# Four single-chunk units at the start, integer addition on VectorE, another order of the gate chain and three more rooms for raw weights, in a linear-attention and SwiGLU kernel

## The chip, the cores and the metric

The kernel runs on one core of one Trainium2 chip. The metric is device microseconds (us) of one execution, as a median of several executions. PE is TensorE, DVE is VectorE, ACT is ScalarE, POOL is GpSimd, SP is SyncE; a "q" behind the name (SPq) marks an instruction that issues a transfer.

## The reference, cut to what matters

```python
# attention: batch 4, heads 8, sequence 768, head size 48, float32
mag = sqrt(a_re**2 + a_im**2)
scale = minimum(mag, 0.999) / (mag + 1e-6)
a_re_n, a_im_n = a_re * scale, a_im * scale
for t in range(S):                                  # complex decay of a state
    new_re = ar * S_re - ai * S_im
    new_im = ar * S_im + ai * S_re
    S_re, S_im = new_re + k[t] outer v[t], new_im
    y[t] = q[t] @ S_re
# feed-forward: 3072 tokens, 384 -> 1536 -> 384
xn = x / sqrt(mean(x * x) + 1e-6) * rms_g
g, val = xn @ w_gate, xn @ w_val                    # weights come as float64
out = (g * sigmoid(g) * val) @ w_out
```

The weights arrive in eight bytes per number and are narrowed on the chip.

## The kernel before

The sequence is cut into 24 chunks of 128 positions. A *unit* is one or two chunks whose gates (magnitude, angle, sine, cosine, running product) DVE and ACT compute together. The rotated k and q are moved by DMA into another layout, PE makes scores, states and outputs, and each double chunk then goes through the feed-forward part (FFN). The weights come in 18 *pieces*: six of w_gate, six of w_val, six of w_out. A raw piece lies in a *room* until ACT and DVE have narrowed it.

The units, one gate chain (shortened), the decays, and the narrowing of a piece:

```python
units = [(0, 1), (1, 1)] + [(n, UC) for n in range(2, N, UC)]    # two of one chunk, then double
...
# gate chain of one unit, each line one step for one engine
yield E("DVE", ..., lambda: tt(im, im, y), K("t0"))              # angle work is mixed in
yield E("DVE", ..., lambda: tt(w, s, r))                         # magnitude
...
yield E("ACT", ..., lambda: act_(out=im, in_=im, func=AF.Arctan), table=["atan"])
yield E("DVE", ..., products, K("p"))                            # running products of the gates
yield E("DVE", ..., sums, K("sums"))                             # running angle
yield E("ACT", ..., lambda: act_(out=r, in_=p, func=AF.Abs_reciprocal_sqrt), table=["ars"])
...
yield E("DVE", ..., [K("k")], lambda t=t: tt(t["k"], t["k"], t["r"]))
yield E("DVE", ..., [K("q")], lambda t=t: tt(t["q"], t["q"], t["p"]))
for i, (o, x, f) in enumerate((("ks", "k", s), ("k", "k", y), ("qs", "q", s), ("q", "q", y))):
    yield E("DVE", ..., lambda ...: tt(t[o], t[x], f), *names)   # four rotation products
...
def decays(...):                                   # a trip through memory, both ways on SyncE
    nc.sync.dma_start(out=dec..., in_=ends[:, u, :, 0:m])
    for a in range(2):
        nc.sync.dma_start(out=t["decay"][a * D:(a + 1) * D, :, 0:m], in_=dec...)
yield step("SP", 1.3, [("p", u)], decays, mb=0.02, then=2.5, queue="rows", ends=[("rows", u)])
...
def total(...):                                    # last step of a weight piece
    nc.gpsimd.tensor_tensor(out=to, in0=part["t"], in1=to, op=ALU.add)
```

No engine's program is written by hand. A small list scheduler inside the kernel, the class `Order`, takes the next step of every lane, estimates when it could begin, emits the earliest, and so fixes the sequence of instructions of each engine when the kernel is built. Its constants are guesses of durations, among them the transfer rate in MB per us:

```python
class Order:
    HOP = 0.06
    ISSUE = 0.6
    LAND = 1.9
    RATE = 0.2
    ...
            if "mb" in more:
                queue = more.get("queue", "rows")
                self.moved[queue] = max(self.moved.get(queue, 0.0), at + 0.4) + more["mb"] / self.RATE
                end = self.moved[queue] + self.LAND
```

## Time and profile before

| | before |
|---|---|
| median of 3 executions | 834.41 us (832.93 to 840.13) |
| span of the profiled run, mean granted clock | 829.0 us, 0.947 |
| first score of chunk 0 / 2 / 4 begins | 43.2 / 138.5 / 177.2 us |
| first gate/value tile of the FFN | 78.6 us |
| last output product ends | 821.9 us |
| PE busy from 200 to 600 | 392.5 of 400 us |

In the page's rows of digits one character stands for a fortieth of the span, about 20.7 us, and a 9 means busy for 90% or more. A timeline line gives start, duration, engine, source line, operation, output and inputs, shapes, count, and in brackets the idle time before it with what ended it.

### The profile page before, as it was taken

What the parts mean: (1) busy time and instruction counts of PE and PEld (TensorE: products, weight loads), DVE (VectorE), ACT (ScalarE), POOL (GpSimd) and SP (SyncE); (2) the same over time, 40 slices, a digit from 0 to 9 for tenths busy, and PEclk for the clock granted to TensorE, in tenths of its full rate; (3) what the DMA queues carried; (4) which work ended last, traced back from release to release, by engine and by line L of the source; (5) the groups of instructions that cost most, each with busy time, mean ns of one, the idle gap of its engine ahead of it and who ended that gap; (6) DMA issues with size and microseconds to landing.
All of it is one profiled execution on the core that took longest, in us unless ns stands there. A gap on an engine that the chain in (4) does not pass through costs nothing.

```text
span 829.0 us, 12028 instructions
## 1 busy us (share of the span) xinstructions
PE 761.3 (92%) x4820; PEld 609.9 (74%) x4820; DVE 428.7 (52%) x709; ACT 360.8 (44%) x565; POOL 79.6 (10%) x103
## 2 busy tenths in 40 slices
PE   5079967989998999999999999999999999999996
PEld 2067845778886878988678888678888778886783
DVE  4656999857775766857784766122211213320220
ACT  5632475557675767767664775111111101110110
POOL 6434432200000000000010000000000000000000
PEclk9556987989998999999999999999999999999999
DMA  8929637562647276554635470045100106200510
GB/s 198 204 54 225 158 114 115 125 113 52 103 96 125 49 127 107 125 74 99 78 106 77 124 116 1 8 97 132 52 0 1 58 13 193 81 1 27 177 63 23
DMA packets 100976, 76.48 MB, mean 92 GB/s; under 512 B 39665, under 2 KB 89585, under 8 KB 100913
## 3 DMA queue, kind: packets, MB, share of 16 engines
q1 hardware_dynamic: 98128, 69.74, 39.9%
q0 software_dynamic: 1920, 5.51, 3.0%
q8 instruction: 40, 0.66, 0.4%
q10 hardware_dynamic: 864, 0.39, 0.2%
q14 instruction: 24, 0.19, 0.1%
HBM read 51.98 MB, written 4.76 MB: 68 GB/s over the span
## 4 chain that ended last, share of the span: by engine, by line
PE 76%; DMA 8%; DVE 7%; ACT 3%; SPq 2%; issue 2%; POOL 1%; DVEq 0%; ACTq 0%; POOLq 0%
PE gv_ps L1160 39%; PE out_ps L1184 20%; PE s_ps L1014 5%; PE y_ps L1087 5%; PE state_ps L1057 3%; SPq L861 2%; DMA hT<-in_w_gate_dram 2%; DMA qr<-q 2%; PE ss_ps L1110 2%; DMA qr<-qs 1%; PE kt_ps L1035 1%; DMA raw<-in_w_gate_dram 1%; DMA dec<-ends 1%; PE ss_ps L1123 1%; DMA raw<-in_w_out_dram 1%
## 5 line engine op out<-in xcount | busy, mean ns | idle before, releaser
L1160 PE MATMUL gv_ps<-xT,wg 128*128 128x256 f32 x864 | 213.8, 384 | 0.2
L1160 PE MATMUL gv_ps<-xT,wv 128*128 128x256 f32 x864 | 210.3, 379 | 0.0
L1184 PE MATMUL out_ps<-wo,hT 128*128 128x384 f32 x576 | 195.9, 493 | 7.8 <-POOL wo L968 7.8
L1160 PEld LDWEIGHTS gv_ps<-xT,wg 128*128 128x128 f32 x864 | 163.5, 192 | 26.1 <-issue 1.4
L1160 PEld LDWEIGHTS gv_ps<-xT,wv 128*128 128x128 f32 x864 | 164.6, 190 | 22.5
L1184 PEld LDWEIGHTS out_ps<-wo,hT 128*128 128x128 f32 x576 | 107.6, 191 | 76.3 <-POOL wo L968 9.6
L612 DVE TENSOR_TENSOR hT<-gv_ps,hT 128x256 f32<-128x256 f32 x144 | 59.6, 421 | 191.3 <-ACT hT L1164 191.0
L1164 ACT ACTIVATE hT<-gv_ps 128x256 f32<-128x256 f32 x144 | 54.1, 383 | 210.4 <-PE gv_ps L1160 209.8
L1014 PE MATMUL s_ps<-qr,kr 96*128 96x128 f32 x384 | 57.0, 310 | 45.3 <-DMA kr<-k 33.0
L1014 PEld LDWEIGHTS s_ps<-qr,kr 96*128 96x128 f32 x384 | 53.0, 221 | 48.7 <-issue 48.6
L1120 POOL TENSOR_TENSOR rs<-ssq,mhalf 128x1 f32<-128x1 f32 x24 | 18.5, 773 | 582.0 <-DVE ssq L1115 582.0
L1193 ACT COPY ot<-out_ps 128x384 f32<-128x384 f32 x24 | 11.5, 480 | 63.8 <-PE out_ps L1184 63.8
L615 DVE SCALAR_TENSOR_TENSOR xT<-y_ps,gcol,rb 128x128 f32<-128x128 f32 x72 | 20.7, 343 | 35.8 <-ACT rb L1128 29.9
L1019 DVE TENSOR_TENSOR am<-s_ps,causal 128x512 f32<-128x512 f32 x48 | 32.1, 683 | 13.2 <-PE s_ps L1014 12.7
L1057 PEld LDWEIGHTS state_ps<-vz,kt 128*96 128x96 f32 x320 | 32.2, 176 | 1.6 <-issue 0.7
L1164 ACT ACT_TABLE_LOAD x25 | 32.1, 1283 | 0.4
L1057 PE MATMUL state_ps<-vz,kt 128*96 128x48 f32 x320 | 32.1, 257 | 0.0
L1128 ACT COPY rb<-ss_ps 128x128 f32<-128x128 f32 x24 | 6.3, 264 | 59.1 <-PE ss_ps L1123 59.1
L1039 ACT COPY kt<-kt_ps 128x384 f32<-128x384 f32 x40 | 17.4, 478 | 26.4 <-PE kt_ps L1035 26.4
L1087 PE MATMUL y_ps<-am,vz 128*32 128x128 f32 x768 | 27.6, 287 | 0.0
L990 DVE TENSOR_REDUCE least__113<-raw 128x1 f32<-128x768 f32 x18 | 17.0, 944 | 20.0 <-DMA raw<-in_w_out_dram 16.2
L1110 PEld LDWEIGHTS ss_ps<-ones,sq 128*128 128x128 f32 x144 | 20.3, 202 | 8.5 <-ACT sq L1105 5.0
(113 smaller groups left out, 818.1 us busy)
## 6 DMA issues: line engine op xcount, KB each, us to landing
raw<-in_w_out_dram SPq DMA_DIRECT2D x12, 768.0 KB, 4.5
k<-in_k_dram SPq DMA_DIRECT2D x24, 192.0 KB, 3.3
q<-in_q_dram SPq DMA_DIRECT2D x24, 192.0 KB, 3.9
vz<-in_v_dram SPq DMA_DIRECT2D x24, 192.0 KB, 4.5
out_dram<-ot SPq DMA_DIRECT2D x24, 192.0 KB, 2.6
raw<-in_w_gate_dram SPq DMA_DIRECT2D x6, 768.0 KB, 4.6
raw<-in_w_val_dram SPq DMA_DIRECT2D x6, 768.0 KB, 4.5
re<-in_a_re_dram SPq DMA_DIRECT2D x33, 128.0 KB, 3.0
```

The costliest lines, as they stand in the source:

```text
L612: nc.vector.tensor_tensor(out=o, in0=x, in1=y, op=op)
L615: nc.vector.scalar_tensor_tensor(out=o, in0=x, scalar=c, in1=y, op0=op0, op1=op1, **kw)
L1014: nc.tensor.matmul(u["s_ps"][a][:, h], lhsT=u["k"][:, a * HH + h], rhs=u["q"][:, a * HH + h], start=True, stop=True)
L1019: nc.vector.tensor_tensor(out=u["am"][a], in0=u["s_ps"][a], op=ALU.mult, in1=causal.unsqueeze(1).to_broadcast([C, HH, C]))
L1039: nc.scalar.copy(out=u["kt"][a], in_=u["kt_ps"][a])
L1057: nc.tensor.matmul(u["st_ps"][:, h], lhsT=u["kt"][h // HH][:, h % HH], rhs=u["v"][:, h, 0:D], start=True, stop=True)
L1087: nc.tensor.matmul(u["y_ps"][32 * p:32 * (p + 1), j], lhsT=columns(left, j, odd, p), rhs=right(h), start=side == 0 and i == 0, stop=side = ...
L1110: nc.tensor.matmul(u["ss_ps"][:, 0:1], lhsT=u["sq"][:, d], rhs=ones, start=d == 0, stop=d == ND - 1)
L1120: nc.gpsimd.tensor_tensor(out=u["rs"], in0=u["ssq"], in1=mhalf, op=ALU.pow)
L1160: nc.tensor.matmul(ps[:, i], lhsT=w_[:, f * P // FW, d, cols], rhs=t["xT"][:, d], start=d == 0, stop=d == ND - 1)
L1164: nc.scalar.activation(out=t["hT"][:, f], in_=t["gv", f][:, 0], func=AF.Silu)
L1184: nc.tensor.matmul(t["o_ps", i], lhsT=t["hT"][:, f, i * C:(i + 1) * C], rhs=wo[:, f], start=f == 0, stop=f == NF - 1)
```

## The change

The intent: chunks 2 and 3 no longer form one double unit but two single ones, so that they can go on through DVE and ACT early. GpSimd no longer adds integers, so it no longer holds up DVE. The products of the gate magnitudes come ahead of the angles, so that k and q are scaled earlier. Raw pieces also use the room of the out-projection weights, which are not there yet. The moves alternate between k and q, three raw pieces instead of six leave at the start, and the scheduler gets one common transfer clock at rate 0.22 in place of one per queue at 0.2. The core of the diff:

```diff
-    RATE = 0.2
+    RATE = 0.22
...
-                queue = more.get("queue", "rows")
-                self.moved[queue] = max(self.moved.get(queue, 0.0), at + 0.4) + more["mb"] / self.RATE
-                end = self.moved[queue] + self.LAND
+                self.moved = max(self.moved, at + 0.4) + more["mb"] / self.RATE
+                end = self.moved + self.LAND
...
-    units = [(0, 1), (1, 1)] + [(n, UC) for n in range(2, N, UC)]
+    ONES = 4
+    units = [(n, 1) for n in range(ONES)] + [(n, UC) for n in range(ONES, N, UC)]
...
+    GL = 0.3
+    GU = (0.0, 0.05, 0.7, 0.7)      # lateness of the gate lanes of units 0 to 3
...
             # gate chain: products first, then angles; k and q scaled ahead of the angle sums
+            yield E("DVE", tt_us(n1), [K("k")], lambda t=t: tt(t["k"], t["k"], t["r"]))
+            yield E("DVE", tt_us(n1), [K("q")], lambda t=t: tt(t["q"], t["q"], t["p"]))
             ... sums, fraction, sine, cosine ...
-            for i, (o, x, f) in enumerate((("ks", "k", s), ("k", "k", y), ("qs", "q", s), ("q", "q", y))):
+            for i, (o, x, f) in enumerate((("ks", "k", s), ("qs", "q", s), ("k", "k", y), ("q", "q", y))):
...
-    EARLY = 6
+    EARLY = 3                       # pieces fetched from GpSimd's queue at the start
...
-        two = (0, 1) if i < 2 else (2, 3) if i < 2 * NW and i % 4 > 1 else (4, 5)
+        k = i if i < 2 else 2 + (i - 2) % 5 if i < 2 * NW else 7 + i % 2    # rooms 4 to 6 lie in wo
...
-                nc.gpsimd.tensor_tensor(out=to, in0=part["t"], in1=to, op=ALU.add)
+                tt(to, part["t"], to, ALU.add)
...
+                        for _ in range(7):           # dummies on rotated data before the first score
+                            nc.tensor.matmul(flat(u["s_ps"][a])[:, 0:ND * C], lhsT=ident, rhs=rotated, ...)
```

## The prediction

> **What bounds the kernel now.** I read the page's table of forty slices first, then the busy times by stretch, then the timelines of TensorE (PE) and VectorE (DVE), then the SyncE queue. From the page:
>
> ```profile
> PE   5079967989998999999999999999999999999996
> DVE  4656999857775766857784766122211213320220
> PEclk9556987989998999999999999999999999999999
> DMA  8929637562647276554635470045100106200510
> ```
>
> A slice is 20.7 us. From the tenth slice on PE is full at full clock; only the first nine show holes and a clock near half. The stretches, with bounds put at stage changes (columns: stretch, its length, busy us of PE, PEld, DVE, ACT, POOL with instruction counts, granted clock, DMA share, GB/s):
>
> ```profile
> 0.00:43.20 43.20, 10.77 (x21) 4.56 (x21) 25.28 (x55) 26.21 (x45) 24.74 (x61) 0.69 0.96 197
> 43.20:78.60 35.40, 30.08 (x201) 24.76 (x202) 18.14 (x27) 9.71 (x17) 13.01 (x9) 0.55 0.61 130
> 78.60:109.60 31.00, 31.00 (x145) 27.31 (x144) 28.83 (x33) 16.19 (x24) 14.15 (x8) 1.00 0.63 154
> 109.60:138.40 28.80, 16.25 (x33) 6.97 (x32) 28.04 (x30) 19.00 (x24) 8.78 (x4) 0.84 0.63 120
> 138.40:177.20 38.80, 36.45 (x299) 29.07 (x299) 29.09 (x46) 24.87 (x36) 4.35 (x3) 0.94 0.63 118
> ```
>
> 43.2 us pass before the first score; 35.4 go into the attention of chunks 0 and 1 at clock 0.55; 31.0 are the first gate/value group, clean; in the next 28.8 PE has nearly nothing to do, while DVE is busy 28.0 of them.
>
> How much useful PE work is there? Warm lengths from PE's timeline: 144 gate/value tiles of 2.6 us (374), 24 output rows of 7.75 (186), 24 score groups of 1.85 (44), 44 output sides of 0.95 (42), 20 states of 1.32 (26), 20 transposes of 0.7 (14), 24 norms of 1.0 (24): **710 us**. By t = 200 these are done: 18 tiles (46.8), 48 of 576 output records at 0.323 (15.5), six scores (11.1), eleven sides (10.4), five states and five transposes (10), the norms (5.5): about **99 us**. So 101 us are lost before 200; afterwards 611 us of work take 622 (200 to 822), a loss of 11, and 7 us are tail. The change can only win from the 101.
>
> The timeline shows what the loss is made of:
>
> ```profile
> 43.17 3.75 PE L1014 MATMUL s_ps<-qr,kr 96*128 96x128 f32 x16 [29.77 <-DMA kr<-k]
> ...
> 116.08 2.92 PE L1184 MATMUL out_ps<-wo,hT 128*128 128x384 f32 x4 [4.99 <-POOL wo L968]
> 121.84 2.27 PE L1184 MATMUL out_ps<-wo,hT 128*128 128x384 f32 x4 [2.83 <-POOL wo L968]
> 123.90 9.77 PE L644 MATMUL s_ps<-causal,ident 128*128 128x512 f32 x20
> 138.45 3.76 PE L1014 MATMUL s_ps<-qr,kr 96*128 96x128 f32 x16 [4.77 <-DMA dec<-ends]
> ```
>
> The first score waits for moved rows and runs cold (3.75 us against 1.98 warm at t = 143). After the first group PE waits for converted out-projection weights, fills with dummy products, and gets chunk 2 only at 138. The cause is on DVE: chunks 2 and 3 are one double unit that begins at 39.5 and shares DVE with all 18 weight pieces.
>
> **What the Trainium skill says, and whether this trace agrees.** (1) "SBUF — State Buffer", Who interferes with whom: a VectorE instruction with two SBUF inputs and a GpSimd one that reads SBUF exclude each other for the whole instruction. Agreed: beside a GpSimd weight addition DVE operations of 0.95 us show two to three times that:
>
> ```profile
> 120.15 2.46 DVE L612 TENSOR_TENSOR k<-k,r 128x768 f32<-128x768 f32 x1
> 122.53 0.95 DVE L612 TENSOR_TENSOR q<-q,p 128x768 f32<-128x768 f32 x1
> ...
> 119.33 2.46 POOL L968 TENSOR_TENSOR wo<-t,wo 128x768 int32<-128x768 int32 x1 [3.30 <-DVE wo L615]
> ```
>
> (2) "TensorE: Matmul & The Clock Gate", What's actually happening: an idle window of about 3.4 us halves the PE clock, a sustained busy one restores it. Agreed: 3.75 against 1.98. The dummies of 2.65 to 13.4 are wasted, since 30 us of idleness follow. (3) "ScalarE: Activation LUTs", What ACT_TABLE_LOAD costs: about 1283 ns a load, plus a drain. The load agrees (25 in the largest group, mean 1283); the drain is no separate row. (4) "DMA: Bandwidth & Descriptors", Issuing engines are not separate DMA queues: all issuers share 16 engines. Agreed: in the first 43 us the share is 0.96 at 197 GB/s, and chunk 0's last move (q) needs 7.3 us behind weight pieces.
>
> **The change part by part.**
>
> *Integer addition on VectorE.* Removes 18 GpSimd additions (1.81 to 2.53 us). Each visibly stretches one DVE operation by about 1.2 to 1.6 us (2.06, 2.17, 2.40, 2.46, 2.57 against 0.55 or 0.95). Adds 18 DVE operations of 0.95 (the row of the `or`, same shape), pitch 0.87. DVE: 18 x (0.9 - 1.3), about -7 us; near even. Latency of a piece falls by about 1 us.
>
> *Four single-chunk units.* Chunks 2 and 3 can begin early, in parallel lanes. Cost: a 384-wide operation has a pitch of 0.47 on DVE, a 768-wide one 0.87, so two singles cost 0.07 more on each of 17 operations: +1.2 us, plus some small scans and copies: +2 us. ACT likewise.
>
> *Gate products ahead of angles.* Chunk 0 loads three tables between 17 and 25.6 before (arctan, reciprocal root, sine); now the root follows while its table is in, and arctan and sine can share one: two of 1.28 saved, about 2.6 us. Work on k and q starts earlier. I put the last rotation of chunk 0 at 25 (28.8 before). Later units save loads too, off the path.
>
> *Transfers.* Three weight pieces instead of six go out early: 2.3 MB less ahead of the moves, 11 us at 200 GB/s; v is postponed; k moves before q. The q move, 4 instead of 7.3 us, no longer starts behind raw pieces. First score: 25 + 2 issue + 5 landing, about **33** instead of 43.2. Three more rooms in the output weights give seven pieces in flight. DMA was nearly idle from 48 to 58 (0 to 2 GB/s in the finer slices), so the postponed pieces have room there.
>
> *Seven dummies on the rotated data* instead of twenty early ones warm PE during the move. Scores through norms of chunks 0 and 1 are about 13 us warm and took 25 (30.1 less 4.9 of dummies). With dependency gaps I expect 20 to 24 us instead of 35.4: first gate/value tile near **55 to 58** instead of 78.6.
>
> *Then weights set the pace.* DVE work until four chunks, all 18 pieces and group 0 are through: 4 units of 11 (two took 22 of the 25.3 busy us before 43.2) = 44; 18 pieces at 0.47 + 0.87 + 0.87 = 40; masks, states and norms 3.15 per chunk = 13; 12 gate products 4.5. Sum **101 us**. DVE starts at 8.3; with 12 us of holes (27 in the same phase before) it is through at about 121. DMA gives the same: 14.2 MB of weights and 1.8 MB for each of four chunks (with moves) are 21.4 MB, 107 us at 200 GB/s.
>
> *The sum.* At 121, PE can have done four chunks (25), group 0 (31) and its output (15.5) = 72 useful us, so 50 are lost. From then on group 1 and two output rows give 46 us of supply, against about 35 for the next double unit (DVE 23, moves and decays 10): no new hole. Total 710 + 50 + 11 + 7 = 778 as the ideal. I add 18 for stalls at handovers, pieces that do not come in the right order, and cold stretches: a span of 796, and 4 for the median's offset from the span (834.4 against 829.0 before): **800 us**. It would be 34 us or 4% less.
>
> **Rivals.** (a) *VectorE becomes the sole bound* between 55 and 120: pieces take 2.2 of DVE, two pieces 4.4 per pair of tiles, which last 5.2 on PE, so group 0 nearly fills DVE and chunks 2 and 3 starve until near 115. For it: DVE is at 28.8 of 31.0 already. Then the hole after group 0 moves rather than closes: loss of 75, 825 us. Against: 20 us of earlier start, during which the extra lanes use idle DVE. (b) *Weights arrive late*: nine pieces wait for chunk 1's rotation, and SyncE issues in order (1.9 us a move, 2 to 2.9 a piece). Group 0 then stretches from 31 to 40: +9, about 810. (c) *The early gain is hidden*: the later chunks arrive no earlier, so the FFN waits later. Then 820 to 830. Against: DVE has 27 idle us before 78.6 that more units can fill. (d) *Everything fits*: 780 to 785.
>
> **Range and chances.** From the ideal 778 plus half the handover allowance to rival (b) plus a partial (a): **784 to 818**. More than 2% faster means below 817.7. Chances: faster 0.86, same 0.12, slower 0.02. Slower would need a later steady state worse than before, which nothing in the change adds.
>
> **What would show each step.** First score at 30 to 36, in about 1.9 us; first gate/value tile before 60; no GpSimd additions and no DVE operations of 2 us and more; chunk 2's score before 110 instead of 138; dummies far fewer near 124; PE full from about 125; DVE idle below 15 us between 8 and 120. It would be wrong if PE still idles 20 us after group 0, if group 0 takes over 45, or if new waits appear past 200, where I assume 18 with the tail, as now.

## The result, and the profile after

| | before | after |
|---|---|---|
| median | 833.67 us (830.48 to 840.13, 4 runs) | 859.00 us (856.78 to 860.44, 4 runs) |
| span, clock of the profiled run | 829.0, 0.947 | 857.9, 0.957 |
| first score of chunk 0 / 1 / 2 / 3 / 4 | 43.2 / 52.0 / 138.5 / 143.2 / 177.2 | 47.7 / 59.5 / 104.9 / 115.0 / 182.1 |
| first / twelfth gate/value tile begins | 78.6 / 107.1 | 81.0 / 151.4 |
| first output row begins | 109.6 | 166.9 |
| last output product ends | 821.9 | 848.7 |

The kernel became slower: the ratio is 1.029 with a 95% interval from 1.022 to 1.036. A ratio is the mean time of one kernel's fast runs over the mean of the other's in the same rounds, so it is not quite the ratio of the medians quoted. Executions over 1.5% slower than the fastest of the same kernel are left out of the means. Results are correct.

The rows of the page of the kernel after (a slice is 21.4 us):

```profile
PE   0265789989998989999998979999999999999995
DVE  2866858957666757575775558323211112320220
PEclk9977879998998999999999989999999999999998
```

PE is not full until the seventh slice (128 us), and there is an 8 in the fifteenth and twenty-second slice and a 7 in the twenty-fourth, between 300 and 515 us, where the kernel before had only 9s. The stretch from 400 to 500 shows that later loss. Columns are stretch, its length, busy us of PE, PEld, DVE, ACT and POOL with counts, granted clock, DMA share and GB/s. First the kernel before, then the kernel after:

```profile
400.00:500.00 100.00, 97.83 (x724) 80.40 (x723) 68.68 (x114) 67.14 (x95) 3.79 (x4) 1.00 0.54 98
```

```profile
400.00:500.00 100.00, 88.78 (x658) 69.47 (x657) 64.65 (x104) 57.42 (x81) 3.54 (x4) 0.97 0.54 100
```

PE lost nine busy us there, and no other engine became busier, nor did the DMA to speak of. That is the mark of waiting, not of more work.

PE's timeline of the kernel after, the lines that answer to those shown of before:

```profile
47.69 3.76 PE L1038 MATMUL s_ps<-qr,kr 96*128 96x128 f32 x16 [4.81 <-DMA kr<-k]
...
80.99 2.77 PE L1184 MATMUL gv_ps<-xT,wg 128*128 128x256 f32 x6
...
102.15 2.93 PE L1184 MATMUL gv_ps<-xT,wv 128*128 128x256 f32 x6 [4.49 <-DVE wv L611]
104.87 3.35 PE L1038 MATMUL s_ps<-qr,kr 96*128 96x128 f32 x16
...
182.07 2.02 PE L1038 MATMUL s_ps<-qr,kr 96*128 96x128 f32 x16 [1.65 <-DMA dec<-ends]
```

The first score is later and still cold, chunk 2 is 34 us earlier, PE waits for a narrowed w_val piece at 102, and chunk 4 is 5 us later than before. The early start of chunk 2 was bought, but what follows it came no earlier.

A measure that sums this up is *useful work by time*: I give every non-dummy PE record of a trace the warm length of its kind in the kernel before (a gate/value tile 2.59 us, an output row 7.75, a score group 1.85, and so on; about 715 us in all) and count what is done by a given time.

| useful us done by | 120 | 160 | 200 | 300 | 400 | 500 | 600 | last product ends |
|---|---|---|---|---|---|---|---|---|
| before | 47 | 67 | 100 | 192 | 292 | 390 | 490 | 821.9 |
| after | 29 | 63 | 95 | 185 | 280 | 367 | 465 | 848.7 |

Up to 120 the kernel after is 18 behind, catches up to 5 behind at 200, and then loses another 20 by 600.

One chain of that later loss, in order of time, from the kernel after. SyncE first sends a unit's results to memory and must wait for them before it fetches them back, then come the next unit's loads:

```profile
472.26 0.57 SPq L890 DMA_DIRECT2D dec<-ends  x1
481.84 2.77 SPq L893 DMA_DIRECT2D decay<-dec  x2
...
489.94 1.01 SPq L740 DMA_DIRECT2D k<-in_k_dram  x2
```

DVE meanwhile stands at the product of k, which the new gate order puts ahead of the angle sums, and behind it stands a gate product that PE's next FFN tile needs:

```profile
494.47 0.96 DVE L611 TENSOR_TENSOR k<-k,r 128x768 f32<-128x768 f32 x1 [6.26 <-DMA k<-in_k_dram]
...
498.65 0.73 DVE L611 TENSOR_TENSOR hT<-gv_ps,hT 128x256 f32<-128x256 f32 x2
```

```profile
499.11 2.93 PE L1184 MATMUL gv_ps<-xT,wg 128*128 128x256 f32 x6 [5.87 <-DVE hT L611]
```

SyncE issued nothing from 472.8 to 481.8, so k was issued at 489.9; DVE stood for 6.3 us and PE for 5.9. The gate product stood only three places behind k on DVE's list (q and the angle sums lie between), and DVE didn't take it out of turn.

### The profile page after: what moved, and what is told of

Read it like the earlier page.

```text
span 857.9 us, 12070 instructions
## 1 busy us (share of the span) xinstructions
PE 763.4 (89%) x4818; PEld 613.5 (72%) x4818; DVE 429.1 (50%) x752; ACT 360.8 (42%) x580; POOL 34.4 (4%) x73
## 5 line engine op out<-in xcount | busy, mean ns | idle before, releaser
L1184 PE MATMUL gv_ps<-xT,wg 128*128 128x256 f32 x864 | 217.0, 388 | 7.0 <-DVE hT L611 7.0
L1184 PE MATMUL gv_ps<-xT,wv 128*128 128x256 f32 x864 | 213.8, 384 | 4.5 <-DVE wv L611 4.5
L1184 PEld LDWEIGHTS gv_ps<-xT,wv 128*128 128x128 f32 x864 | 166.9, 193 | 28.3 <-DVE wv L611 4.9
L1038 PEld LDWEIGHTS s_ps<-qr,kr 96*128 96x128 f32 x384 | 54.9, 227 | 23.5 <-issue 22.4
L1144 POOL TENSOR_TENSOR rs<-ssq,mhalf 128x1 f32<-128x1 f32 x24 | 16.5, 686 | 701.0 <-DVE ssq L1139 701.0
L1035 PE MATMUL s_ps<-ks,ident 128*128 128x384 f32 x14 | 6.1, 602 | 36.7 <-DVE ks L611 36.7
L1081 PEld LDWEIGHTS state_ps<-vz,kt 128*96 128x96 f32 x320 | 29.7, 165 | 7.2 <-ACT kt L1063 6.0
L1081 PE MATMUL state_ps<-vz,kt 128*96 128x48 f32 x320 | 30.2, 247 | 4.3 <-ACT kt L1063 4.3
L1063 ACT COPY kt<-kt_ps 128x384 f32<-128x384 f32 x40 | 17.5, 480 | 34.9 <-PE kt_ps L1059 34.9
L1035 PEld LDWEIGHTS s_ps<-ks,ident 128*128 128x128 f32 x14 | 3.3, 242 | 39.0 <-issue 37.9
L1009 DVE TENSOR_REDUCE least__113<-raw 128x1 f32<-128x768 f32 x18 | 17.0, 947 | 27.9 <-DMA raw<-in_w_out_dram 17.5
L1188 ACT ACT_TABLE_LOAD x23 | 29.5, 1283 | 0.4
```

The costliest lines, as they stand in the source:

```text
L1009: nc.vector.tensor_reduce(out=least_[:, i:i + 1], in_=words(raws.pop(i))[1].bitcast(FP32), axis=mybir.AxisListType.X, op=ALU.min, apply_ab ...
L1038: nc.tensor.matmul(u["s_ps"][a][:, h], lhsT=u["k"][:, a * HH + h], rhs=u["q"][:, a * HH + h], start=True, stop=True)
L1063: nc.scalar.copy(out=u["kt"][a], in_=u["kt_ps"][a])
L1081: nc.tensor.matmul(u["st_ps"][:, h], lhsT=u["kt"][h // HH][:, h % HH], rhs=u["v"][:, h, 0:D], start=True, stop=True)
L1144: nc.gpsimd.tensor_tensor(out=u["rs"], in0=u["ssq"], in1=mhalf, op=ALU.pow)
L1184: nc.tensor.matmul(ps[:, i], lhsT=w_[:, f * P // FW, d, cols], rhs=t["xT"][:, d], start=d == 0, stop=d == ND - 1)
```

## The experiments

The theory after reading the traces was that the change is not slow in its operations but in its *order*: the engines' lists are laid out for times that the chip does not keep, so that engines wait at the head of their lists while other work is ready. Rivals were that one of the new pieces (VectorE's addition, the gate order, the late weights, the late imaginary gates, four units) costs the time by itself. "Same order" below means that the edit leaves every other instruction where it was; the other edits let the scheduler lay out a new order. An edit is against the kernel after unless the text says the kernel before. Every profiled run was correct; each kernel had three rounds and is compared with the kernel before of its own rounds. The intervals of the ratios are 0.005 to 0.012 wide to each side, 4 to 10 us, so a gain of some 5 us alone is not clear of noise.

### First set: one suspect each

**a1s_im.** In the kernel after, ACT issues the im transfers of units 0 and 1 behind its first square, which waits for re. The two lines of ACT's timeline of the kernel after:

```profile
4.57 4.47 ACTq L724 DMA_DIRECT2D im<-in_a_im_dram  x6
12.93 0.52 ACT L790 ACTIVATE w<-im 128x384 f32<-128x384 f32 x1 [7.86 <-DMA im<-in_a_im_dram]
```

The kernel before issued the first of them at 0.80 and had its square of im at 7.73. The edit issues im with re, same order otherwise:

```diff
+            def both(ap, queue, u=u, gate=gate):
+                gate("re", ap, queue)
+                gate("im", a_im, nc.scalar)
```

> The changed kernel, same order on every engine but one: the imaginary gates of units 0 and 1 are issued from ScalarE before its first activation, instead of behind an activation that waits for the real gates (in the changed kernel they were issued at 4.6 us and the first VectorE operation began at 13.5 us, against 8.3 us before). Theory (head of line on in-order queues): first VectorE operation near 8.5, first score near 43 instead of 47.7, end 3 to 5 us earlier than 859 if the head start survives to the weights. Rival (the start is hidden behind the late weights): first operation earlier, end within 2 us of 859.

Measured: 853.91 us, ratio 1.025 [1.017, 1.034]. The first score came at 41.2 instead of 47.7, the first FFN tile at 73.5 instead of 81.0, and the whole kernel ended 5 us earlier by the medians (3 by the ratios, whose intervals overlap). The late im is real at the start; what it is worth at the end is within noise, and it is not the cause of the loss.

**a2s_kq.** The products of k and q are emitted just ahead of the first rotation product, same order otherwise:

```diff
-            yield E("DVE", tt_us(n1), [K("k")], lambda t=t: tt(t["k"], t["k"], t["r"]))
-            yield E("DVE", tt_us(n1), [K("q")], lambda t=t: tt(t["q"], t["q"], t["p"]))
+            def rotate(i, o, x, f, t=t):
+                if i == 0:
+                    tt(t["k"], t["k"], t["r"])
+                    tt(t["q"], t["q"], t["p"])
+                tt(t[o], t[x], f)
```

> The changed kernel, same order on every engine except that VectorE's products of k and q with the gates stand just ahead of the first rotation, as before the change, so that nothing queued behind them waits for the load of k. Theory (VectorE blocked by k's load, 5.7 and 6.3 us in two units seen, delays masks, states and gate products that PE waits for): the time after 200 us falls, end at 838 to 850. Rival (the loss after 200 us comes from the schedule's shape, not from these waits): within 4 us of 859.

Measured: 849.57 us, 1.021 [1.014, 1.029]. PE was busy 97.6 us of the stretch from 400 to 500 instead of 88.8, and DVE's waits for k (11.9 us in two) were gone. So the chain shown above is real. By the medians the edit is worth 9 us of the 25, by the ratios 6, with intervals that overlap.

**a3s_fetch.** Raw pieces 3 to 6 are issued from SyncE earlier, same order otherwise:

```diff
+                if u == 3 and name == "im":
+                    ahead(3); ahead(4)
+                if u == 0:                  # between the two halves of the decays' trip
+                    ahead(5); ahead(6)
```

> The changed kernel, same order on every engine except that weight pieces 3 to 6 (whose rooms are free from the start) are issued on SyncE at about 29 us and in front of the first decay's wait, instead of at 68 to 84 us. Theory (weights come late because SyncE issues them in order behind moves and waits): first gate/value tiles no longer wait for pieces, ScalarE no longer idles 7 us for piece 3, chunk 1's norm is ready near 71 instead of 79; end 6 to 12 us earlier, about 850. Rival (VectorE's static order sets the pace anyway): within 3 us of 859.

Measured: 854.18 us, 1.026 [1.018, 1.034], between theory and rival and within noise of the kernel after. Chunk 1's moves were delayed behind the pieces (its score came at 68.0 instead of 59.5). The narrowing of the fourth to eighth piece came no earlier. Late weights are not cured by issuing a few of them earlier.

**b1_add.** The kernel before with the integer addition on DVE and nothing else:

```diff
-                nc.gpsimd.tensor_tensor(out=to, in0=part["t"], in1=to, op=ALU.add)
+                tt(to, part["t"], to, ALU.add)
```

> The kernel before with the integer addition on VectorE alone (and so modelled in its scheduler). Theory: near even on VectorE, 18 operations of 0.95 us added and about 18 stretches of 1.2 to 1.6 us removed: 826 to 834 us. Rival (the added VectorE work costs while VectorE is full, 60 to 140 us): 838 to 850 us.

Measured: 828.53 us, 0.998 [0.990, 1.006]. The addition is harmless and worth next to nothing.

### Second set: sums and parts

**c1_all3** is the three same-order edits together.

```diff
+            def both(ap, queue, u=u, gate=gate): ...          # as in a1s_im
+            def rotate(i, o, x, f, t=t): ...                  # as in a2s_kq
+                    ahead(3); ahead(4)                        # as in a3s_fetch, with 5 and 6
```

> The changed kernel with the three same-order corrections at once (imaginary gates issued first, products of k and q just ahead of the rotations, weight pieces 3 to 6 issued early). Each alone gave 5, 9.5 and 5 us. Theory (three separate head-of-line waits): they add, 838 to 843 us, so about 20 of the 25 us that the change lost. Rival (they hide the same wait): 847 to 850.

Measured: 849.17 us as the median of three fast executions (840.71, 849.17 and 850.22; a fourth took 1598.35 us), 1.016 [1.004, 1.028]. This does not decide whether they add. Alone they were 5, 9 and 5 us better by the medians, together 10; by the ratios they sum to 0.015 and gave 0.013 together, with an interval that holds both answers.

**d1_early6.** Six early pieces instead of three, and 0.03 instead of 0.0 as unit 0's lateness, so the scheduler lays out everything anew:

```diff
-    GU = (0.0, 0.05, 0.7, 0.7)
+    GU = (0.03, 0.05, 0.7, 0.7)
-    EARLY = 3
+    EARLY = 6
```

> The changed kernel with six weight pieces sent early on GpSimd's queue, as before the change, and the tie on ScalarE broken the other way so that the imaginary gates are issued first; the scheduler knows of both and lays out a new order. Theory (three pieces early instead of six is what makes group 0 end at 152 instead of 110, and chunks 4 and 5 come late behind it): group 0 ends before 130 and the end is 835 to 845. Rival (VectorE's work for four chunks is what stretches group 0): group 0 still ends after 140, end 850 or more.

Measured: 843.55 us, 1.015 [1.007, 1.022]. The end lies where the theory put it, but group 0 was not through before 130: the twelfth gate/value tile began at 137.4 (151.4 in the kernel after). So six early pieces and an early im, with the order that comes with them, are worth some 12 us by the ratios. By 120 its useful work was 44, nearly the kernel before's 47, and it still ended 10 us later.

**d2_ones2.** The kernel after with two single units, as before, and all the rest of the change:

```diff
-    ONES = 4
+    ONES = 2
-        ... else ("rot", 3) if i >= 2 * NW else None
+        ... else ("rot", ONES - 1) if i >= 2 * NW else None
```

> The changed kernel with two single-chunk units instead of four (chunks 2 and 3 a double unit again); everything else of the change stays. Theory (the four units are not the harm; the order of the gate chain and the late weights are): 850 to 862. Rival (the four units, that put 44 us of gate work ahead of the weights on VectorE, are the harm): 835 to 845.

Measured: 833.91 us, 1.002 [0.995, 1.010]. The rival was right: with these constants, two single units more are the difference between even and 3% slower. The order is a new one here too, so the run doesn't part the units' own cost from that of the order.

**b2_gates.** The kernel before with the new order of the gate chain (products first, k and q ahead of the sums):

```diff
+            ... products, p -> reciprocal root -> square -> ks, r -> k*r, q*p
             ... then arctangent, sums, fraction, sine, cosine
```

> The kernel before with the changed order of the gate chain alone (products ahead of angles, products of k and q ahead of the sums; rotations and moves as before). Theory (this order is the harm in the steady state, as moving the products of k and q back gave 9.5 us): 840 to 848, lost after 200 us. Rival (it is harmless by itself): 828 to 836.

Measured: 833.24 us, 1.002 [0.994, 1.009]. The gate order alone is harmless. So neither the addition nor the gate order costs anything by itself. That k ahead of the sums hurts only where k is late is how I read this beside a2s_kq.

### Third set: the wait on SyncE, and the order itself

**e1_dec.** The decays' trip is issued from GpSimd, so that its wait blocks no load; same order:

```diff
-                nc.sync.dma_start(out=dec..., in_=ends[:, u, :, 0:m])
+                nc.gpsimd.dma_start(out=dec..., in_=ends[:, u, :, 0:m])
-                    nc.sync.dma_start(out=t["decay"]..., in_=dec...)
+                    nc.gpsimd.dma_start(out=t["decay"]..., in_=dec...)
```

> The changed kernel, same order on every engine except that the two-step trip of the decays through memory (out of VectorE's ends, back into the decay tile) is issued from GpSimd's queue, idle in the changed kernel, so that SyncE no longer waits 7 to 10 us in it with the loads of the next unit behind. Theory (SyncE's wait for the decays delays the next unit's loads, and with them k, the gate chain and at last PE): the loads come 8 us sooner per unit, end 838 to 848. Rival (the loads are not what the gate chain waits for): 856 to 862.

Measured: 828.56 us, 0.996 [0.991, 1.001]. By the ratios (1.029 - 0.996, of some 833 us) this one edit is worth 27 us, the whole loss, and more than the theory expected. The view of waits (engine and line, what for, us in total, times, longest) over the whole run; first the kernel after, then e1_dec:

```profile
SPq L893 <- DMA dec<-ends: 96.8, 14, 9.1
...
DVE k L611 <- DMA k<-in_k_dram: 11.9, 2, 6.3
```

```profile
POOL decay L893 <- DMA dec<-ends: 79.5, 14, 9.2
...
DVE k L611 <- DMA k<-in_k_dram: 0.6, 1, 0.6
```

The trip still takes its time, but GpSimd has little else to do (34.4 us busy in the kernel after), and DVE's wait for k is gone as well. The edit also takes the trip's issuing off SyncE, about 20 us over the run (14 times 0.59 and 28 times 0.42). A rival would be that the trip merely lands sooner from the other queue. PE's waits for transfers ahead of scores don't show it: 17.5 us in the kernel after, 16.3 in e1_dec. How the wait reaches the weights is seen in SyncE's issues, first of the kernel after, then of e1_dec:

```profile
112.20 1.32 SPq L890 DMA_DIRECT2D dec<-ends  x1
116.79 1.23 SPq L893 DMA_DIRECT2D decay<-dec  x2
...
121.95 2.00 SPq L952 DMA_DIRECT2D hT<-in_w_gate_dram  x4
```

```profile
104.02 1.83 SPq L878 DMA_DIRECT2D qr<-raw  x3
105.94 1.87 SPq L724 DMA_DIRECT2D re<-in_a_re_dram  x3
...
109.78 3.49 SPq L952 DMA_DIRECT2D hT<-in_w_gate_dram  x4
```

The ninth raw piece left 12.2 us earlier without the two trips of units 2 and 3 in between. Between 80 and 120 the DMA moved 151 GB/s instead of 111.

**e2_add_dec.** The kernel before with the addition on DVE and the trip on GpSimd (the edits of b1_add and e1_dec).

```diff
-                nc.sync.dma_start(out=dec..., in_=ends[:, u, :, 0:m])
+                nc.gpsimd.dma_start(out=dec..., in_=ends[:, u, :, 0:m])     # and both of t["decay"]
-                nc.gpsimd.tensor_tensor(out=to, in0=part["t"], in1=to, op=ALU.add)
+                tt(to, part["t"], to, ALU.add)
```

> The kernel before with the addition on VectorE and the decays' trip on GpSimd's queue. Theory (SyncE's wait matters there as well): 815 to 824, faster than the kernel before by over 1%. Rival (before hides that wait): 826 to 832, as with the addition alone (828.5).

Measured: 820.44 us, 0.989 [0.982, 0.995]. The theory's figure came. The same move of the trip is worth about 1% (0.998 to 0.989, from two sets, with intervals that overlap) here, against 3.3% in the kernel after. SyncE waits for these transfers in both (83.4 us in 13 times before, 96.8 in 14 after); so the length of the wait alone doesn't tell its cost. That it depends on what stands behind it in the list is argued here.

**e3_dec_im_kq** is e1_dec with the edits of a1s_im and a2s_kq, same order.

```diff
+                nc.gpsimd.dma_start(out=dec..., in_=ends[:, u, :, 0:m])     # as in e1_dec
+            def both(ap, queue, u=u, gate=gate): ...                         # as in a1s_im
+            def rotate(i, o, x, f, t=t): ...                                 # as in a2s_kq
```

> The changed kernel with three same-order corrections: decays' trip on GpSimd's queue, imaginary gates first, products of k and q just ahead of the rotations. Theory (in-order waits make up the loss, and add): 828 to 838. Rival (k's wait and SyncE's wait are one and the same, and what remains is the order laid out for times that the chip does not keep): 841 to 848.

Measured: 825.81 us, 0.994 [0.989, 0.998]. With the trip off SyncE, the other two, worth 5 and 9 us alone by the medians, add less than 3 us. That fits the view that most of what they gained was loss by the same delay.

**t1_rate15.** The kernel after with one constant of the scheduler changed, and the trip still on SyncE:

```diff
-    RATE = 0.22
+    RATE = 0.15
```

> The changed kernel with one number of its scheduler changed: transfers at 0.15 instead of 0.22 MB per us, near what the trace moves in the first 160 us (137, 141, 111, 176 GB/s). The scheduler then expects chunk 2 at 101 and chunk 4 at 167 instead of 86 and 152; the chip gave 105 and 182. Theory (the fixed order was laid out for transfers that the chip does not make, so engines wait in order with other work queued behind): 838 to 850. Rival (the order is near enough, the work itself is late): 855 to 865.

Measured: 824.48 us, 0.992 [0.986, 0.998]. This is better than the theory's range. No operation, size or queue differs from the kernel after, only the sequence and twelve more records of dummy products (60 against 48), which the scheduler puts into the gaps that it expects. SyncE waits as long as it did; its view of waits has this line:

```profile
SPq L893 <- DMA dec<-ends: 97.3, 14, 9.3
```

Yet PE is full in the late stretch, where it had been busy for 88.8 us:

```profile
400.00:500.00 100.00, 99.93 (x646) 83.03 (x645) 66.00 (x105) 64.08 (x94) 2.53 (x2) 1.00 0.65 102
```

One difference is the place of the ninth raw piece. In this order it stands ahead of unit 3's moves and leaves at 101.06 instead of 121.95.

### What the scheduler expected, against the chip

The scheduler's own times can be read while the kernel is built. I set the end of the narrowing of the 18 weight pieces, sorted by time, against the traces. The cells give chip less expectation, in us:

| piece | 3rd | 6th | 8th | 9th | 12th | 18th | rate | ratio |
|---|---|---|---|---|---|---|---|---|
| before | 7 | 19 | 18 | 17 | 16 | 18 | 0.20 | 1 |
| after | 15 | 21 | 21 | 30 | 32 | 35 | 0.22 | 1.029 |
| g3_rate18 (told below) | 10 | 12 | 12 | 22 | 23 | 30 | 0.18 | 1.014 |
| e1_dec | 16 | 19 | 19 | 20 | 21 | 20 | 0.22 | 0.996 |
| t1_rate15 | 6 | 12 | 12 | 10 | 8 | 5 | 0.15 | 0.992 |
| g2_rate15_dec_im (told below) | 1 | 8 | 7 | 5 | 4 | 1 | 0.15 | 0.977 |

A lateness that is the same for all steps would merely shift an order. In the two slow kernels (after and g3_rate18) it jumps by 9 or 10 us between the eighth and the ninth piece, where two trips block SyncE. In e1_dec, with the same expectations as the kernel after, the jump is gone. The table supports the theory but does not measure it fully: d2_ones2 is level with the kernel before, though its out-projection pieces also grow later by 10 us and more (its narrowing of w_out came at 163 to 214, and one record is missing there). The scheduler expected PE's last product at 798 (before), 786 (after) and 810 (t1_rate15); the chip gave 821.9, 848.7 and 814.1. The order that promised most delivered least.

### Fourth set: are the two remedies one, and does before gain too

**g1_rate15_dec** has rate 0.15 and the trip on GpSimd.

```diff
-    RATE = 0.22
+    RATE = 0.15
-                nc.sync.dma_start(out=dec..., in_=ends[:, u, :, 0:m])
+                nc.gpsimd.dma_start(out=dec..., in_=ends[:, u, :, 0:m])     # and both of t["decay"]
```

> The changed kernel with the scheduler's transfer rate at 0.15 and the decays' trip on GpSimd's queue (each alone gave 824.5 and 828.6). Theory (two causes: an order laid out for too early times, and SyncE's waits that make the times late): some gain over either, 812 to 821. Rival (both cure the same misfit, and the order for late times gains nothing from earlier loads): 822 to 830.

Measured: 823.17 us, 0.984 [0.977, 0.991]. By the medians that is 1.3 us better than t1_rate15, by the ratios 0.8% (two sets and two chips, so I don't tell these apart). Alone the two remedies are worth 27 and 31 us by the ratios; together 38. They remove nearly the same loss.

**g2_rate15_dec_im** adds the edit of a1s_im to g1_rate15_dec.

```diff
+            def both(ap, queue, u=u, gate=gate):
+                gate("re", ap, queue)
+                gate("im", a_im, nc.scalar)
```

> As the one before, with the imaginary gates of units 0 and 1 issued ahead of ScalarE's first activation as well (same order otherwise). Theory (the early stages start some 6 us sooner and the order does not need to change): 808 to 818. Rival (the order for late times swallows it): within 2 us of the run without it.

Measured: 818.75 us (814.82 to 820.22), 0.977 [0.970, 0.984]. It is the best form of the change. First score 44.9, first FFN tile 72.6, chunk 4 at 168.8.

**g3_rate18** is the kernel after with rate 0.18.

```diff
-    RATE = 0.22
+    RATE = 0.18
```

> The changed kernel with the scheduler's transfer rate at 0.18 MB per us, between 0.22 (859) and 0.15 (824.5). Theory (the misfit shrinks with the rate): between, 830 to 850. Rival (any other order would have done, the one at 0.22 is bad luck): 820 to 829, or over 859.

Measured: 850.31 us, 1.014 [1.007, 1.022]. With 859.0 at 0.22 and 824.5 at 0.15 there is a trend, but not a smooth one.

**g4_before_rate15** is the kernel before with rate 0.15.

```diff
-    RATE = 0.2
+    RATE = 0.15
```

> The kernel before with the scheduler's transfer rate at 0.15 instead of 0.2. Theory (its order fitted the chip already, at 0.2 for each queue on its own): 826 to 838, within 1% of before. Rival (every order of this scheduler gains from the lower rate): 815 to 824.

Measured: 825.1 us, 0.986 [0.979, 0.993]. The kernel before also gains from an order for slower transfers, though less than half as much.

### Fifth set: the change against a kernel before with the same remedies

**h1_before_fit.** The kernel before with the addition on DVE, the trip on GpSimd and rate 0.15.

```diff
-    RATE = 0.2
+    RATE = 0.15
+                nc.gpsimd.dma_start(out=dec..., in_=ends[:, u, :, 0:m])     # and both of t["decay"]
+                tt(to, part["t"], to, ALU.add)
```

> The kernel before with the addition on VectorE, the decays' trip on GpSimd's queue and the scheduler's rate at 0.15: what the kernel before gives when it has the same corrections as the best form of the change (818.75 us, 0.977 of before). Theory (with the misfit gone, four single-chunk units and the other rooms are worth little): 812 to 820, level with it. Rival (the change is worth its 10 us once its order fits): 822 to 830.

Measured: 817.65 us (813.46 to 820.45), 0.980 [0.972, 0.987]. This is level with g2_rate15_dec_im.

**h2_ones2_fit.** g2_rate15_dec_im with two single units instead of four (the edit of d2_ones2).

```diff
-    ONES = 4
+    ONES = 2
```

> The best form of the change (rate 0.15, decays' trip on GpSimd's queue, imaginary gates first: 818.75 us) with two single-chunk units instead of four. Theory (once the order fits, the four units do what they were made for: chunk 2 at 105 instead of some 125 to 130, PE fed sooner): 822 to 832, so the four units are worth 4 to 13 us there, though they cost 25 us in the order at 0.22. Rival (the four units cost in any order): 808 to 817.

Measured: 821.07 us, 0.985 [0.979, 0.991]. Against g2_rate15_dec_im (0.977) the intervals overlap: once the order fits, four units are not told apart from two.

| useful us done by | 120 | 200 | 300 | 600 | last product ends |
|---|---|---|---|---|---|
| before | 47 | 100 | 192 | 490 | 821.9 |
| h1_before_fit | 44 | 104 | 205 | 505 | 807.2 |
| g2_rate15_dec_im | 46 | 111 | 202 | 503 | 809.3 |
| h2_ones2_fit | 43 | 103 | 203 | 502 | 810.9 |

No form of the change has more done at 120 than the kernel before. The best ones, like h1_before_fit, gain between 160 and 300 and lose nothing afterwards.

## Why the prediction was wrong, point by point

- **The bound and the place of the loss** in the kernel before were read rightly: PE is the bound after 200, and the early 100 us were open. What was wrong is what the change would make of them. Two small readings were wrong as well: the DMA was idle from 52 to 58 (0 to 10 GB/s), not from 48 (99 and 66 GB/s from 48 to 52), and PE's thirteenth slice is an 8, from a wait of 4.0 us for a move.
- **Integer addition.** Right: 18 operations on DVE of 0.95 us, no GpSimd additions, and the stretched DVE operations are gone. b1_add gives 0.998. The rows of the costliest groups, before and then after, show the stretched sum of the double units back at the length of its shape. (One of the eleven took 5.33 us beside two additions, more than the 1.2 to 1.6 that the prediction allowed for a stretch.)

```profile
L612 DVE TENSOR_TENSOR s<-s,w 128x768 f32<-128x768 f32 x11 | 16.5, 1498 | 4.8 <-ACT w L776 4.8
```

```profile
L611 DVE CUSTOM_DVE_ANT_0 wg<-t,wg 128x1536 uint16<-128x1536 uint16 x6 | 5.7, 958 | 0.2
...
L611 DVE TENSOR_TENSOR s<-s,w 128x768 f32<-128x768 f32 x10 | 9.6, 957 | 1.7 <-ACT w L790 1.7
```

- **Gate chain and first score.** Wrong: 47.7 instead of 33. DVE's first operation is at 13.5 (8.3 before), since im is issued behind ACT's wait for re. a1s_im takes 6.5 us of that back; the best form has 44.9. Of the 8 us that then remain (41.2 against 33), the trace of a1s_im has 6 before the end of chunk 0's last rotation (31.2, forecast 25), where DVE also runs steps of chunk 1 and of a weight piece, and 3 in its moves (9.9, forecast 7). The saving of table loads did not come: ahead of chunk 0's rotation ACT loads four tables instead of three, and 67 instead of 69 in all, each 1283 ns.
- **Dummies.** Wrong: 48 records against 50 before (each dummy product is two records, so the seven new ones are 14 against 20 early ones). They ended at 42.9, PE then idled 4.8 us, and the first score ran at a clock of 0.50. First score to first FFN tile took 33.3 us, not 20 to 24.
- **Four units.** Chunk 2 before 110 was right (104.9). But chunk 4 came at 182.1 instead of 177.2, so the earlier start passed nothing on.
- **Weights.** The mechanism of rival (b), pieces late behind SyncE's issues in order, is what the traces show. Its size was wrong: I gave it 9 us of group 0, and the twelfth gate/value tile came at 151.4, 44 us later than before. SyncE's wait inside the decays' trip, 96.8 us over the run, did not appear in my list of issue times at all. Rival (a) is not what happened: DVE was busy 31.4 of the 40 us from 80 to 120. Rival (c), that the later chunks come no earlier, fits chunk 4, but its 820 to 830 was too low as well.
- **The step that failed is "The sum"**, with "Then weights set the pace" under it. It put 72 useful us at 121; the kernel after had 29 at 120, and its best form 46. The step took DVE's 101 us and the DMA's 107 us as work that is handed over almost without gaps in the order in which it is needed. DVE had 101 busy us behind it at 151 instead of 121, so it stood 41 us where the step allowed 12 (the view is below this list), and even then five of the 18 pieces were still to be narrowed. From 121 on the step expected no new hole; PE did 66 useful us in the 80 from 120 to 200. The 18 us of allowance were to cover the order of the pieces; that term was mis-sized by far.
- **"No new loss after 200"** (I gave "slower" a chance of 0.02) failed as well, and with it "slower would need a later steady state worse than before, which nothing in the change adds". At 200 the kernel after had 95 of 715 done, so 620 were left; they took 648.7 us (200 to 848.7), a loss of 29 against 7 by the same measure before (615 in 621.9). What added it is the sequence: the changed constants and lanes lay out every list anew, up to the end, and I read the diff for operations and not for what it does to the order. Two of my three signs of being wrong came: group 0 took 73 us instead of at most 45 (81.0 to 154.1), and there were new waits past 200.

DVE's share of the stretch from its forecast start to 151 in the kernel after (columns as above, so DVE is the third busy time):

```profile
8.30:151.00 142.70, 90.78 (x591) 72.66 (x592) 101.38 (x194) 83.47 (x136) 12.87 (x24) 0.86 0.71 142
```

What the runs show as the cause: the loss needs this order *and* the wait on SyncE. Taking away either (t1_rate15, e1_dec) removes 31 or 27 us, both remedies together 38, and two units instead of four, again with a new order, removes 22. Six early pieces instead of three, with im first and a new order, remove 12. No part of the change that I ran alone in the kernel before costs anything (b1_add, b2_gates); four units, the rooms and the early pieces were not run alone there. The expected gain of 34 us is not hidden behind the loss: with the same remedies on both sides, 0.977 and 0.980 are level.

What is argued and not shown: why exactly the trip costs 3.3% in the order of four units and 1% in the order before. The places of k, of the ninth piece and of the decays in the lists are instances, not a full account. Part of the 31 us of t1_rate15 may be what the lower rate gives the kernel before too (0.986, some 12 us). Open also remains how much of each rate's result is luck of one order among many: a small change of one constant reshuffles all lists, and 0.22, 0.18 and 0.15 are only three of them.

Of the versions run, h1_before_fit (817.65) and g2_rate15_dec_im (818.75) beat both kernels by about 2% of the kernel before.

## What to carry to other kernels

When a kernel's instruction order comes from an estimate, every change of an operation or a constant is also a change of the order: compare the expected with the measured times first, and run each part alone with the order held. A transfer that waits for another transfer belongs on a queue where nobody waits behind it. Before you credit an early start, ask which supply (weights, loads, vector work) the next stage waits for, and test the change against a kernel before that has had the same remedies.

## What the Trainium skill lacked or had wrong

- "DMA: Bandwidth & Descriptors", Issuing engines are not separate DMA queues, says that issuing from several engines saves only the time of issuing. Here three small transfers per unit (one out, two back) moved from SyncE to GpSimd took 27 us off the kernel (e1_dec, by ratio): the way back waits for the way out and held up the loads behind it, 96.8 us of SyncE's time in 14 waits. The page does say that the issuing engine has to wait for the first of two dependent transfers, but not that this counts when the queue is chosen.
- The same page, Latency and other measured facts, gives about 800 ns as the least round trip to memory. The transfer of 3 KB that opens the decays' trip took 9.0 us in the median until it landed, issued from SyncE behind twelve moves, and 4.6 us from GpSimd. For the 1.5 KB transfers of the single units it was the other way round, 4.4 and 7.8 us. The page has no figure for the landing of small transfers among traffic.
- "TensorE: Matmul & The Clock Gate", What's actually happening, has the full clock back after about 3.4 us of sustained work and puts the ramp below 1% of a typical span. In the kernel before, PE was busy without a gap from 52.0 to 60.1 us and the granted clock stayed at 0.50, so the prediction's "Agreed" under its point (2) is true of the score's length only; the six wide dummies from 73.8 were followed by 1.00 at 78.6. From 43.2 to 78.6 the clock was 0.55. By my estimate this cost some 12.6 us (30.1 busy us less 4.9 of dummies, halved), about 1.5% of 829. Why the first stretch did not bring the clock up is not shown.
- "DVE: scalar operands, raw-bit mode, write accounting and state across instructions", Scalar operands, says that DVE's ALU is float32, so that an int32 pointer scalar is not exact past 2^24. The trace shows the int32 tensor addition as one custom operation on 1536 uint16 halves in 0.96 us, as long as a float32 operation of 768 elements, with correct results. No page that I read tells that this form exists or what it costs.
